# Last units of the first batch ahead of three weight tiles and of the second batch's maxima

## The chip, the core and the metric

The kernel runs on one core of one Trainium2 chip. The metric is the device time of one execution in microseconds. Before the change three runs took 1084.18 us (median), 1084.15 and 1089.09. TensorE (PE) does the matmuls, VectorE (DVE), ScalarE (ACT) and GpSimd (POOL) the elementwise work, SyncE (SP) issues nearly all DMAs. Each engine takes its instructions in the order in which they stand in its own queue.

## The reference

Attention over a window of 32 neighbours, with 32 global tokens, in 8 batches of 8 heads, 512 local tokens, 64 columns per head; then two matrices with a softplus between them, in float32:

```python
s_g = scale * q_g @ k_all.T          # 32 global tokens against all 544 keys
out_g = softmax(s_g) @ v_all
s_l = concat(scale * q_l @ k_g.T,    # each local token: 32 global keys ...
             where(abs(i - j) <= 32, scale * q_l @ k_l.T, -1e9))   # ... and its window
out_l = softmax(s_l) @ concat(v_g, v_l)
x = concat(out_g, out_l)             # 4352 rows of 512 (8 heads x 64)
h = x @ w_in                         # 512 x 2048
g = max(h, 0) + log1p(exp(-abs(h)))
out = g @ w_out                      # 2048 x 512
```

## The kernel before

**Precision.** A float32 operand is split into a high half, stored as float32r (`xh`, `gh`, the first half of a weight tile) and the remainder (`xl`, `gl`, the second half). Each product is three matmuls: high by high, low by high, high by low.

**First batch.** Batch 0 is done by special steps: for each pair of heads m = 0 to 3 and each half a = 0, 1 a local unit, and two global units between them, ten in all (`steps`). A unit goes through seven functions: `scores0` (matmuls, row maximum, exponential), `invert0`, `diag0`, `turn0`, `evict0`, `values0` (matmuls into a PSUM bank `o0_m_a` of the pool `ps_h`, which has two banks), `split0` (reads this bank: ScalarE casts it to `xh`, line L226, and VectorE subtracts to `xl`, L228). A global unit ends with ScalarE's copy to `yg` (L269). The loop over k from -2 to n + 1 (n = 10) runs units in a pipeline: in iteration k unit k + 2 begins and unit k - 2 ends.

**Weight tiles.** The weights come as 32 tiles, `wi0` to `wi15` and `wo0` to `wo15`, in the order of `order_w`: wi0, wi1, wi2, wi3, wo0, wo1, wi4, wi5, wo2, wo3, wi6, wi7, wo4, wo5, wi8 and so on. They arrive as 64-bit floats, and each is made into two halves: ScalarE's `abs_w` (L479), four VectorE operations in `bits_w` (L486, L488, L489, L492), ScalarE's cast (L497) and GpSimd's subtraction (L498). In the loop above one tile is prepared per iteration (`held`: `abs_w` in one, the rest in the next), the first twelve (`W_PRE`) of them. The rest follow between the products, when `weights(upto)` is called with a growing number.

**Other batches.** The pairs of heads m = 4 to 31 are cut into pieces with a place on one scale (`pieces`): three `scores(m, p)` at 12m + 4p, three `values(m, p)` at 22 more, `invert` and `normalise` behind them. The piece of the third `scores` also holds `maxima(m)` (GpSimd copies L329, VectorE L332 to L339) and three `probs(m, q)` (VectorE's transpose to `mb`, L347, GpSimd's subtractions L352 to L355, ScalarE's exponential L356). The pool tag `mb` has two buffers, which `abs_w` also uses for tiles below 8. The loop places the pieces of m = 4 and 5 below a limit among its last four iterations; the rest are taken after each product, as far as their place goes.

**Products.** `moe_items` puts for each batch and each of 16 blocks f the first product `h` (`hpart`, into the two `ps_h` banks), `act` (softplus: ScalarE L540 to L542, VectorE's L543, which is the last to read the `h` bank, `gh` on ScalarE, `gl` on GpSimd, L547) and the second products `o` a block or two behind. `split_x` makes `xh` and `xl` (L451, L452) of a later batch at its start; parts 1 and 3 are VectorE's.

**Order.** The program is written in one sequence, and a scheduler then orders each engine's queue by the sequence and its own estimates. In the loop, a few chains (`keep`, `note`) are forced into the written order. The single `a` bank of `ps_a` is shared by the scores of m = 6 on (`s_ps`) and by `values` (`v_ps`); VectorE's L374 and L375 are the last to read a `v_ps`.

Of the kernel before, what the change touches and what calls it, by code (L numbers as in the profile page):

```python
# [23 lines left out]
NPC = 3  # L24
# [6 lines left out]
M0 = 4  # L31
# [5 lines left out]
W_PRE = 12  # L37
START = 69
# [9 lines left out]
def windows(ap2d, start, stride, count, width):  # L48
    base = ap2d[:, start:start + width]
    return bass.AP(base.tensor, base.offset, [list(base.ap[0]), [stride, count], [1, width]])  # L50
# [3 lines left out]
def moe_over_global_local_attention(  # L54
# [219 lines left out]
    def load(m, p):  # L274
        w = QW[p] + KWID[p]
        raw = pl.tile([P, 544], F32, tag="raw", name=f"raw{m}_{p}", bufs=3)
        order["load"] = nc.sync.dma_start(out=raw[:, :w], in_=qk[m - M0, :, EW[p]:EW[p] + w]).ins
        st["raw", m, p] = raw

    def load_v(m):  # L280
        t = pl.tile([P, 2, 6, 66], F32, tag="v", name=f"v{m}", bufs=2)
        nc.gpsimd.memset(t[:, :, :, D:D + 1], 1.0)
        nc.sync.dma_start(out=t[:, :, :, 0:D], in_=v[m - M0].rearrange("p (h c d) -> p h c d", h=2, d=D))
        st["v", m] = t
# [35 lines left out]
    def grid(t, start, *dims):  # L320
        base = t[0:32, start:start + 1]
        return bass.AP(base.tensor, base.offset, [list(base.ap[0])] + [list(d) for d in dims])
# [3 lines left out]
    def maxima(m):  # L326
        mt = st.pop(("mt", m))
        for a in range(1, 4):
            nc.gpsimd.tensor_copy(mt[0:32, GW * a:GW * a + GW], mt[32 * a:32 * a + 32, 0:GW])  # L329
        e0 = 4 * GW  # L330
        for u, du, off in ((0, 1, -2), (3, 1, 3)):
            nc.vector.tensor_reduce(grid(mt, e0 + u, (7, 6), (du, 2)), grid(mt, 3 + u, (12, 6), (du, 2), (off, 2), (GW, 4)), axis=AX.XY, op=ALU.max)  # L332
        nc.vector.tensor_reduce(grid(mt, e0 + 2, (7, 6), (4, 2)), grid(mt, 3 + 2, (12, 6), (7, 2), (GW, 4)), axis=AX.X, op=ALU.max)
        g = e0 + 44
        nc.vector.tensor_reduce(grid(mt, g, (1, 2)), grid(mt, 3 + 5, (36, 2), (12, 3), (3, 2), (GW, 4)), axis=AX.XYZ, op=ALU.max)
        nc.vector.tensor_copy(grid(mt, e0 + 5, (21, 2), (7, 3)), mt[0:32, g:g + 2].unsqueeze(2).to_broadcast([32, 2, 3]))
        e = mt[:, e0:e0 + 44]
        for a in range(1, 4):
            i = nc.vector.tensor_copy(e[32 * a:32 * a + 32, 0:42], e[0:32, 0:42]).ins  # L339
        order["maxima"] = i  # L340
        st["e", m] = e

    def probs(m, p):
        s, e = st["s", m, p], st["e", m]
        k = QW[p] // 32
        mb = pl.tile([P, 2, 288], F32, tag="mb", name=f"mb{m}_{p}", bufs=2)
        nc.vector.transpose(mb[:, :, :QW[p]].rearrange("p h (s k) -> p h s k", k=32),  # L347
                            windows(e, 7 * p, 21, 2, k).unsqueeze(3).to_broadcast([P, 2, k, 32]))
        for h in range(2):
            if p < 2:  # L350
                sw = s[:, h].rearrange("p (c w) -> p c w", w=192)
                nc.gpsimd.tensor_tensor(sw, sw, windows(mb[:, h], 0, 96, 2, 192), op=ALU.subtract)  # L352
        if p == 2:
            nc.gpsimd.tensor_tensor(s[:, :, 0:192], s[:, :, 0:192], mb[:, :, 0:192], op=ALU.subtract)
            nc.gpsimd.tensor_tensor(s[:, :, 192:288], s[:, :, 192:288], mb[:, :, 96:192], op=ALU.subtract)  # L355
        nc.scalar.activation(s, s, AF.Exp, scale=0.125)  # L356

    def values(m, p):
        s, vt = st.pop(("s", m, p)), st["v", m]
        ps = ps_a.tile([P, 2, 512], F32, tag="a", name=f"v_ps{m}_{p}")  # L360
        parts = ((0, 0, 192), (192, 96, 192 if p < 2 else 96))
        for h in range(2):
            for i, (o, qs, w) in enumerate(parts):
                mm(ps[:65, h, qs:qs + w], lhsT=vt[:, h, 2 * p + i, 0:65], rhs=s[:, h, o:o + w],
                   start=i == 0, stop=i == 1, skip_group_check=True)

        if p == 0:
            st["x", m] = pl.tile([65, 2, 608], F32, tag="x", name=f"x{m}", bufs=2)
            nc.scalar.copy(st["x", m][:, :, 0:288], ps[0:65, :, 0:288])
            return  # L370
        x, o = st["x", m], XOFF[p]
        w = QW[p] if p < 2 else 160
        nc.scalar.copy(x[:, :, o + 64:o + w], ps[0:65, :, 64:w])
        nc.vector.tensor_tensor(x[:, :, o:o + 64], x[:, :, o:o + 64], ps[0:65, :, 0:64], op=ALU.add)  # L374
        nc.vector.tensor_tensor(x[:, :, 160:192], x[:, :, 160:192], ps[0:65, :, 160:192], op=ALU.add)  # L375
# [5 lines left out]
    def combine(m):  # L381
        nc.sync.dma_start(out=rec_dram[2 * m:2 * m + 2], in_=st["x", m][64:65])

        rows = rec_dram[2 * m:2 * m + 2].rearrange("h (s k) -> (h s) k", k=32)
        sc = pl.tile([38, 32], F32, tag="sc", name=f"sc{m}", bufs=1)
        nc.sync.dma_start(out=sc, in_=rows)
        st["sc", m] = sc, rows

    def invert(m):
        sc, rows = st.pop(("sc", m))  # L390
        after(nc.vector.tensor_scalar(sc, sc, 1e-9, None, op0=ALU.add), "scores")
        nc.vector.reciprocal(sc, sc)
        nc.sync.dma_start(out=rows, in_=sc)
        rb = pl.tile([64, 2, 608], F32, tag="rb", name=f"rb{m}", bufs=1)
        r = rec_dram[2 * m:2 * m + 2]
        nc.sync.dma_start(out=rb, in_=r.unsqueeze(0).to_broadcast([64, 2, 608]))
        st["rb", m] = rb

    def normalise(m):
        b, j = divmod(m, H // 2)  # L400
        x, rb = st.pop(("x", m)), st.pop(("rb", m))
        y = xa[b, j] = pl.tile([P, 608], F32, tag="xa", name=f"xa{b}_{j}", bufs=4)
        for h in range(2):
            after(nc.vector.tensor_tensor(y[64 * h:64 * h + 64], x[0:64, h], rb[:, h], op=ALU.mult), "scores")  # L404
        nc.sync.dma_start(out=xg_dram[j, :, SG * b:SG * b + SG], in_=y[:, 160:192])
        ready.add((b, j))

    def end(m):
        return 12 * m + 8 + LAG

    def pieces():
        def piece(*fs):
            def go():
                for f in fs:
                    f()
            return go
        ps = []
        for m in range(M0, M):
            for p in range(NPC):
                fs = [lambda m=m, p=p: scores(m, p)]  # L420
                if m + 1 < M:
                    fs.append(lambda m=m, p=p: load(m + 1, p))
                if p == 2:
                    fs.append(lambda m=m: maxima(m))
                    fs += [lambda m=m, q=q: probs(m, q) for q in range(NPC)]
                ps.append((12 * m + 4 * p, piece(*fs)))
                fs = [lambda m=m, p=p: values(m, p)]
                if p == 2:
                    fs.append(lambda m=m: combine(m))
                    if m + 2 < M:  # L430
                        fs.append(lambda m=m: load_v(m + 2))
                    ps.append((end(m) + STEP, lambda m=m: invert(m)))
                    ps.append((end(m) + 2 * STEP, lambda m=m: normalise(m)))
                ps.append((12 * m + 4 * p + LAG, piece(*fs)))
        ps.sort(key=lambda t: t[0])
        return ps
# [170 lines left out]
    wk = [0, 0]  # L607
# [23 lines left out]
    pcs = pieces()  # L631
# [5 lines left out]
    n = len(steps)  # L637

    def stage(k, f):
        if 0 <= k < n:  # L640
            steps[k][0][f](*steps[k][1])

    tight, held = True, None
    for k in range(-2, n + 2):
        stage(k + 2, 0)

        while k >= n - 2 and pcs[0][0] < min(12 * M0 + 8 * (k - n + 3), START):
            pcs.pop(0)[1]()
        if k == 0:
            key_masks()  # L650
        if held:
            r = bits_w(*held)
        stage(k + 2, 1)
        stage(k - 2, 5)
        stage(k - 2, 6)
        stage(k, 3)
        stage(k, 4)
        stage(k + 2, 2)
        if held:
            halves_w(*held[:2], r)  # L660
            held = None
        if -1 <= k and wk[1] < W_PRE:
            held = order_w[wk[1]]
            held += (abs_w(*held),)
            wk[1] += 1
# [78 lines left out]
```

## Time and profile before

| | |
|---|---|
| median of three runs | 1084.18 us (1084.15 to 1089.09) |
| profiled execution: time | 1085.38 us |
| profiled execution: span from first to last instruction | 1083.2 us |
| mean granted TensorE clock | 0.973 |
| TensorE busy | 1020.1 us (94%) |
| VectorE, ScalarE, GpSimd busy | 599.8, 546.8, 460.3 us |

Times in the rows are microseconds from the span's start. A row of the timeline gives start, length, engine, line, operation, what is written and read (names without buffer numbers), shape, and in brackets the idle time just before and what ended it. TensorE's ends are modelled, so a busy TensorE need not run at its peak; the granted clock says how fast it was allowed to go.

### The profile page before, as it was taken

The page shows a single profiled execution, that of the slowest core. Times are in us where ns is not written, and L with a number is a line of the kernel's source. Part 1 is how long each engine was busy: PE and PEld are TensorE (multiplying, and loading weights), DVE is VectorE, ACT ScalarE, POOL GpSimd, SP SyncE. Part 2 cuts the span into 40 slices and gives each one's busy share as a digit, 9 for nine tenths or more (in the row PEclk, how much of TensorE's full clock was granted, in tenths as well). Part 3 has the DMA queues.
Part 4 walks back from the last instruction along what each step waited for, and adds up shares of the span by engine and source line. Part 5 has one row for each costly group of instructions (what it writes and reads, how often), then busy time and mean ns, then how long its engine had stood idle before and what let it go on. Part 6 is the DMA issues. An engine that isn't in the chain of part 4 may idle for free.

```text
span 1083.2 us, 14191 instructions
## 1 busy us (share of the span) xinstructions
PE 1020.1 (94%) x5108; PEld 806.4 (74%) x5108; DVE 599.8 (55%) x1138; ACT 546.8 (50%) x968; POOL 460.3 (42%) x526
## 2 busy tenths in 40 slices
PE   6896789899999999999999999999999999999996
PEld 4774567677777777777777777777777778888895
DVE  5988697875455655565555645565556652311211
ACT  6855556544445544545444544554554544454452
POOL 2236475652444444444444344444445442322221
PEclk8998889999999999999999999999999999999998
DMA  9532332313121212123122312122122210100010
GB/s 363 161 101 88 112 129 70 93 47 95 46 57 50 85 52 57 48 56 96 48 56 57 94 47 57 48 81 57 49 55 57 85 28 13 57 15 1 1 40 19
DMA packets 78565, 75.05 MB, mean 69 GB/s; under 512 B 53380, under 2 KB 57476, under 8 KB 78496
## 3 DMA queue, kind: packets, MB, share of 16 engines
q1 hardware_dynamic: 77952, 74.09, 23.1%
q8 instruction: 40, 0.66, 0.3%
q14 instruction: 29, 0.24, 0.1%
q10 hardware_dynamic: 544, 0.07, 0.0%
HBM read 64.43 MB, written 9.71 MB: 68 GB/s over the span
## 4 chain that ended last, share of the span: by engine, by line
PE 74%; DVE 7%; DMA 4%; issue 3%; POOL 2%; ACT 1%; DVEq 0%; POOLq 0%; ACTq 0%
PE h L126 31%; PE o L126 30%; PE v_ps L126 8%; PE s_ps L126 5%; DMA rb<-rec_scratch 2%; DVE xa L404 1%; DVE xl L452 1%; DMA rec_scratch<-sc 1%; POOL s L352 1%; DVE xh L451 1%; DVE s L315 1%; POOL wo L498 0%; DVE mb L347 0%; DVE wbitswo L489 0%; DVE wbitswo L486 0%
## 5 line engine op out<-in xcount | busy, mean ns | idle before, releaser
L126 PE MATMUL h<-xh,wi 128*128 128x512 f32 (+1 forms) x1152 | 357.6, 394 | 23.1 <-DVE xl L228 9.2
L126 PE MATMUL o<-wo,gh 128*128 128x512 f32 x1088 | 348.0, 401 | 0.0
L547 POOL TENSOR_TENSOR gl<-e,gh 128x512 fp32r<-128x512 f32 x136 | 177.2, 1303 | 397.1 <-ACT gh L546 352.3
L126 PEld LDWEIGHTS h<-xh,wi 128*128 128x128 f32 x1152 | 208.8, 190 | 71.8 <-issue 16.1
L126 PEld LDWEIGHTS o<-wo,gh 128*128 128x128 f32 x1088 | 202.4, 190 | 44.3 <-issue 3.8
L126 PE MATMUL h<-xl,wi 128*128 128x512 f32 (+1 forms) x576 | 220.8, 383 | 2.8 <-DVE xl L452 2.8
L126 PE MATMUL o<-wo,gl 128*128 128x512 f32 x544 | 215.3, 396 | 0.0
L540 ACT ACTIVATE e<-h 128x512 f32<-128x512 f32 x136 | 81.4, 598 | 264.5 <-PE h L126 258.8
L543 DVE SCALAR_TENSOR_TENSOR e<-h,e 128x512 f32<-128x512 f32 x136 | 93.2, 685 | 183.6 <-ACT e L542 183.6
L352 POOL TENSOR_TENSOR s<-s,mb 128x384 f32<-128x384 f32 x112 | 138.8, 1270 | 14.0 <-DVE mb L347 14.0
L546 ACT CAST gh<-e 128x512 fp32r<-128x512 f32 x136 | 84.2, 619 | 94.2 <-DVE e L543 94.1
L126 PEld LDWEIGHTS h<-xl,wi 128*128 128x128 f32 x576 | 109.5, 190 | 27.5 <-DVE xl L452 5.6
L126 PEld LDWEIGHTS o<-wo,gl 128*128 128x128 f32 x544 | 103.5, 190 | 23.2
L126 PE MATMUL v_ps<-s,v 128*65 128x192 f32 (+1 forms) x672 | 116.6, 317 | 4.0 <-DVE s L315 3.6
L126 PEld LDWEIGHTS v_ps<-s,v 128*65 128x65 f32 x672 | 90.7, 140 | 28.3 <-DVE s L315 4.1
L315 DVE TENSOR_TENSOR s<-s_ps,mask 128x768 f32<-128x768 f32 (+1 forms) x96 | 64.9, 696 | 82.7 <-PE s_ps L126 82.7
L542 ACT ACTIVATE e<-e,one 128x512 f32<-128x512 f32 x136 | 98.5, 724 | 3.3
L356 ACT ACTIVATE s<-s 128x768 f32<-128x768 f32 (+1 forms) x84 | 66.6, 792 | 65.5 <-POOL s L352 51.4
L126 PE MATMUL s_ps<-raw 64*128 64x192 f32 (+1 forms) x672 | 78.6, 347 | 11.4 <-issue 6.8
L541 ACT ACTIVATE e<-e 128x512 f32<-128x512 f32 x136 | 85.7, 630 | 3.4
L126 PEld LDWEIGHTS s_ps<-raw 64*128 64x128 f32 x672 | 53.2, 188 | 42.4 <-issue 33.0
L316 DVE TRANSPOSE_TENSOR_REDUCE mt<-s 128x24 f32<-128x768 f32 (+1 forms) x84 | 76.2, 908 | 11.4 <-ACT s L311 9.3
(144 smaller groups left out, 831.2 us busy)
## 6 DMA issues: line engine op xcount, KB each, us to landing
raw<-in_qk SPq DMA_DIRECT2D x56, 272.0 KB
v<-in_v SPq DMA_DIRECT2D x28, 384.0 KB
out<-ot SPq DMA_DIRECT2D x34, 256.0 KB
rb<-rec_scratch SPq DMA_DIRECT2D x28, 304.0 KB
wiraw<-in_w_in SPq DMA_DIRECT2D x16, 512.0 KB
woraw<-in_w_out SPq DMA_DIRECT2D x16, 512.0 KB
raw<-in_qk SPq DMA_DIRECT2D x28, 224.0 KB
v<-in_v SPq DMA_DIRECT2D x4, 512.0 KB
```

The lines of the kernel that those rows point to most:

```text
L126: order["pe"] = after(nc.tensor.matmul(*a, **k), "pe").ins
L315: nc.vector.tensor_tensor(s[:, :, o:o + w], ps[:, :, o:o + w], mk.unsqueeze(1).to_broadcast([P, 2, w]), op=ALU.add)
L316: order["scores"] = nc.vector.tensor_reduce(windows(mt, 3 + 12 * p, 36, 2, nb), s.rearrange("p h (b k) -> p h b k", k=32), axis=AX.X, op=A ...
L352: nc.gpsimd.tensor_tensor(sw, sw, windows(mb[:, h], 0, 96, 2, 192), op=ALU.subtract)
L356: nc.scalar.activation(s, s, AF.Exp, scale=0.125)
L404: after(nc.vector.tensor_tensor(y[64 * h:64 * h + 64], x[0:64, h], rb[:, h], op=ALU.mult), "scores")
L540: nc.scalar.activation(e, ph, AF.Abs)
L541: nc.scalar.activation(e, e, AF.Exp, scale=-1.0)
L542: nc.scalar.activation(e, e, AF.Ln, bias=one)
L543: nc.vector.scalar_tensor_tensor(e, ph, 0.0, e, op0=ALU.max, op1=ALU.add)
L546: nc.scalar.copy(gh, e)
L547: nc.gpsimd.tensor_tensor(gl, e, gh.bitcast(F32), op=ALU.subtract)
```

## The change

It makes three edits. The piece of the third `scores` loses `maxima` and `probs`, which become a piece of their own half a place later (12m + 8.5). The loop places only pieces with a whole place, so the maxima of m = 4 and 5 are left for the first call behind the loop's end. And a weight tile is begun in iterations 0 to 8 in place of -1 to 10: nine tiles, wi0 to wo2; wo3, wi6 and wi7 are left for `weights`, which reaches them in the second block of batch 0.

```diff
+                ps.append((12 * m + 4 * p, piece(*fs)))
                 if p == 2:
-                    fs.append(lambda m=m: maxima(m))
-                    fs += [lambda m=m, q=q: probs(m, q) for q in range(NPC)]
-                ps.append((12 * m + 4 * p, piece(*fs)))
+                    fs = [lambda m=m: maxima(m)] + [lambda m=m, q=q: probs(m, q) for q in range(NPC)]
+                    ps.append((12 * m + 4 * p + 0.5, piece(*fs)))
...
-        while k >= n - 2 and pcs[0][0] < min(12 * M0 + 8 * (k - n + 3), START):
-            pcs.pop(0)[1]()
+        if k >= n - 2:
+            for pc in [pc for pc in pcs if pc[0] < min(12 * M0 + 8 * (k - n + 3), START) and pc[0] % 1 == 0]:
+                pcs.remove(pc)
+                pc[1]()
...
-        if -1 <= k and wk[1] < W_PRE:
+        if 0 <= k < n - 1 and wk[1] < W_PRE:
```

TensorE's queue holds the same instructions in the same order in both programs. Three places in the other queues follow.

VectorE at the end of the first batch, before. `mt_763` are the maxima of m = 5 and `mb_0_839` the first transpose made from them; `wbitswi_798` is wi6, `wbitswi_1011` and `_1057` are wi8 and wi9; the last row is the last local unit's `split0`:

```order
L335 TENSOR_REDUCE mt_763<-mt_763 32x2
L486 TENSOR_SCALAR wbitswi_798<-wbitswi_798 128x512
L336 COPY mt_763<-mt_763 32x6
L488 TENSOR_SCALAR wbitswi_798<-wbitswi_798 128x512
L339 COPY mt_763<-mt_763 32x42 x3
L486 TENSOR_SCALAR wbitswi_1011<-wbitswi_1011 128x512
L489 SCALAR_TENSOR_TENSOR wbitswi_798<-wiraw_160,wbitswi_798 128x512
L486 TENSOR_SCALAR wbitswi_1057<-wbitswi_1057 128x512
L347 STREAM_TRANSPOSE mb_0_839<-mt_763 128x576
L488 TENSOR_SCALAR wbitswi_1011<-wbitswi_1011 128x512
L492 SCALAR_TENSOR_TENSOR wiraw_160<-wiraw_160,wbitswi_798 128x512
L228 TENSOR_TENSOR xl_3_780<-o_3_1_858,xh_3_779 64x256 x2
```

And now, where `mb_2_851` is the third transpose of m = 4 and `mt_728` the maxima of m = 5:

```order
L316 TENSOR_REDUCE mt_728<-s_2_786 128x2x9
L347 STREAM_TRANSPOSE mb_2_851<-mt_647 128x2x192
L228 TENSOR_TENSOR xl_3_745<-o_3_1_791,xh_3_744 64x256 x2
L332 TENSOR_REDUCE mt_728<-mt_728 32x6x2 x2
L333 TENSOR_REDUCE mt_728<-mt_728 32x6x2
L335 TENSOR_REDUCE mt_728<-mt_728 32x2
L336 COPY mt_728<-mt_728 32x6
L339 COPY mt_728<-mt_728 32x42 x3
L486 TENSOR_SCALAR wbitswi_1011<-wbitswi_1011 128x512
```

The last unit's L228 has moved ahead of the maxima of m = 5, of wi6 and of the first operations of wi8 and wi9. On ScalarE L226 has likewise moved ahead of two `abs_w`, and L269 to the place right behind the second exponential of m = 4.

GpSimd behind the first batch, before (`gl_0` to `gl_2` are low halves of blocks 0 to 2, `wi_891` is wi7, `wi_1017` wi8, `wo_959` wo4, `wi_1063` wi9, `wo_991` wo5, `wo_1103` wo6):

```order
L498 TENSOR_TENSOR wi_891<-wiraw_162,wi_891 128x512
L547 TENSOR_TENSOR gl_0_921<-e_0_915,gh_0_920 128x512
L498 TENSOR_TENSOR wi_1017<-wiraw_894,wi_1017 128x512
L498 TENSOR_TENSOR wo_959<-woraw_164,wo_959 128x512
L498 TENSOR_TENSOR wi_1063<-wiraw_896,wi_1063 128x512
L498 TENSOR_TENSOR wo_991<-woraw_166,wo_991 128x512
L547 TENSOR_TENSOR gl_1_950<-e_1_944,gh_1_949 128x512
L498 TENSOR_TENSOR wo_1103<-woraw_898,wo_1103 128x512
L547 TENSOR_TENSOR gl_2_1006<-e_2_1000,gh_2_1005 128x512
```

And now (`wi_926` and `wi_935` are wi6 and wi7, `mt_971` the maxima of m = 6):

```order
L547 TENSOR_TENSOR gl_1_950<-e_1_944,gh_1_949 128x512
L498 TENSOR_TENSOR wi_926<-wiraw_160,wi_926 128x512
L547 TENSOR_TENSOR gl_2_1006<-e_2_1000,gh_2_1005 128x512
L498 TENSOR_TENSOR wi_935<-wiraw_162,wi_935 128x512
L282 MEMSET v_1123 128x12
L498 TENSOR_TENSOR wi_1017<-wiraw_815,wi_1017 128x512
L498 TENSOR_TENSOR wo_959<-woraw_164,wo_959 128x512
L498 TENSOR_TENSOR wi_1063<-wiraw_817,wi_1063 128x512
L547 TENSOR_TENSOR gl_3_1092<-e_3_1086,gh_3_1091 128x512
L498 TENSOR_TENSOR wo_991<-woraw_166,wo_991 128x512
L498 TENSOR_TENSOR wi_1173<-wiraw_1009,wi_1173 128x512
L329 COPY mt_971<-mt_971 32x75 x3
```

The weight halves have moved behind the first low halves `gl`, and the copies for the maxima of m = 6 stand behind wi7, wi8, wo4, wi9, wo5 and wi10 (`wi_1173`).

VectorE at the start of batch 2, before (`xa_3` is the last part of the new `x`, `mb_2` the third transpose of m = 13, `s_ps_0` the scores of m = 14); the starts of batches 3 to 6 read alike:

```order
L404 TENSOR_TENSOR xa_3_3037<-x_2790,rb_3004 64x608 x2
L451 CAST xh_3_3071<-xa_3_3037 128x128
L451 CAST xh_3_3071<-xa_3_3037 128x384
L452 TENSOR_TENSOR xl_3_3072<-xa_3_3037,xh_3_3071 128x128
L347 STREAM_TRANSPOSE mb_2_2981<-mt_2823 128x2x192
L452 TENSOR_TENSOR xl_3_3072<-xa_3_3037,xh_3_3071 128x384
L315 TENSOR_TENSOR s_0_3048<-s_ps_0_3041,mask 128x768
```

And now:

```order
L404 TENSOR_TENSOR xa_3_3037<-x_2790,rb_3004 64x608 x2
L347 STREAM_TRANSPOSE mb_2_2996<-mt_2823 128x2x192
L451 CAST xh_3_3071<-xa_3_3037 128x128
L451 CAST xh_3_3071<-xa_3_3037 128x384
L452 TENSOR_TENSOR xl_3_3072<-xa_3_3037,xh_3_3071 128x128
L315 TENSOR_TENSOR s_0_3048<-s_ps_0_3041,mask 128x768
L452 TENSOR_TENSOR xl_3_3072<-xa_3_3037,xh_3_3071 128x384
```

The third transpose stands ahead of the casts, and the larger part of `xl` behind the masking of the next scores.

## The prediction

> **What bounds the kernel now.** I read the page's share of busy time first, then the clock line, then busy time by stretch, then the timeline of each engine where TensorE stands still.
>
> ```profile
> PE 1020.1 (94%) x5108; PEld 806.4 (74%) x5108; DVE 599.8 (55%) x1138; ACT 546.8 (50%) x968; POOL 460.3 (42%) x526
> 80.00:155.00 75.00, 51.83 (x238) 38.25 (x238) 60.49 (x97) 43.76 (x75) 43.20 (x44) 0.86 0.32 107
> 155.00:220.00 65.00, 58.55 (x270) 44.90 (x269) 56.21 (x94) 36.10 (x60) 41.50 (x39) 0.90 0.30 88
> 220.00:1083.00 863.00, 842.51 (x4180) 671.59 (x4178) 419.17 (x810) 412.74 (x679) 355.37 (x405) 0.99 0.19 52
> ```
>
> The first row is the page's. The others give a stretch, its length, busy time of PE, PEld, DVE, ACT and POOL, the granted clock, and DMA. TensorE (PE) fills 94% of the span, and after 220 us it is idle 20.5 us in 863. From 80 to 155 us it is idle 23.2 us in 75 and its clock is down to 0.86. So TensorE bounds the kernel, and what can be won lies at its start. In that stretch VectorE (DVE) is busy 60.5 of 75 us: its free time, 14.5 us, limits how far everything behind it can move forward.
>
> The order of TensorE's own instructions is the same in both programs. Only VectorE, ScalarE (ACT) and GpSimd (POOL) change places, and on SP's queue one small store of `xa`, that nothing in this part waits for, goes behind one load. A gain or loss can therefore come only from TensorE's waits.
>
> ```profile
> 80.06 0.43 PE L126 MATMUL o0g<-p0g1gl,v 32*128 32x64 f32 x2
> 89.72 1.19 PE L126 MATMUL h<-xh,wi 128*128 128x512 f32 x2 [9.23 <-DVE xl L228]
> 94.16 1.46 PE L126 MATMUL v_ps<-s,v 128*65 128x192 f32 x8
> 97.22 0.72 PE L126 MATMUL h<-xh,wi 128*128 128x512 f32 x2 [1.60 <-ACT yg L269]
> 100.18 0.59 PE L126 MATMUL s_ps<-raw 64*128 64x192 f32 x4
> 112.28 0.73 PE L126 MATMUL h<-xh,wi 128*128 128x512 f32 x2 [3.41 <-DVE e L543]
> 118.53 1.01 PE L126 MATMUL s_ps<-raw 64*128 64x192 f32 x4 [4.48 <-issue]
> 154.67 1.01 PE L126 MATMUL s_ps<-raw 64*128 64x192 f32 x4 [4.10 <-ACT wo L497]
> ```
>
> Start, length, and in brackets the idle time before and its end. The longest wait, 9.23 us, is for L228: the first `h` tile takes the PSUM bank of the last local unit's `o`, which L228 still has to read. The 1.60 us are the same thing for the second `h` tile and the global unit's `yg`. The waits at 112, 118 and 154 us end when VectorE gets round to reading a bank (`e`, or the `x` additions), behind weight tiles in its queue.
>
> **The change, part by part.** *The weight tiles begin one step later.* In the first steps a tile's four VectorE operations stand between two steps:
>
> ```profile
> 13.51 0.17 DVE L173 TENSOR_SCALAR sums<-sums 128x4 f32<-128x4 f32 x1 [1.95 <-ACT e L167]
> 14.90 0.17 DVE L165 TENSOR_SCALAR sums<-sums 128x4 f32<-128x4 f32 x1
> 15.78 0.43 DVE L486 TENSOR_SCALAR wbitswi<-wbitswi 128x512 f32<-128x512 f32 x1 [0.71 <-ACT wbitswi L479]
> 17.43 0.69 DVE L492 SCALAR_TENSOR_TENSOR wiraw<-wiraw,wbitswi 128x512 int32<-128x512 int32 x1
> 18.04 0.16 DVE L173 TENSOR_SCALAR sums<-sums 128x4 f32<-128x4 f32 x1
> ```
>
> From 15.78 to 18.04 a tile takes 2.26 us, with 0.71 before it. A step without a tile waits 1.95 us for ScalarE's exponentials, so the step after the row at 14.90 (ends 15.07) goes on at 17.0 and not at 18.04: 1.0 us; the later steps keep their tile, of lower number, and get the rest back. I take 2.0 us of lead at the end of the front, with 1.0 and 2.8 as bounds. DMA hides under it: the load order stands.
>
> *The last unit ahead of wi6 and of the second maxima (m = 5).*
>
> ```profile
> 79.56 0.54 DVE L347 STREAM_TRANSPOSE mb<-mt 128x384 f32<-128x384 f32 x1
> 82.30 0.53 DVE L332 TENSOR_REDUCE mt<-mt 32x12 f32<-32x96 f32 x2 [2.20 <-POOL mt L329]
> 87.33 1.48 DVE L492 SCALAR_TENSOR_TENSOR wiraw<-wiraw,wbitswi 128x512 int32<-128x512 int32 x1
> 88.73 0.85 DVE L228 TENSOR_TENSOR xl<-o,xh 64x256 fp32r<-64x256 f32 x2
> 79.52 0.84 ACT L356 ACTIVATE s<-s 128x768 f32<-128x768 f32 x1 [2.75 <-POOL s L352]
> 82.73 0.73 ACT L226 CAST xh<-o 64x256 fp32r<-64x256 f32 x2
> 96.74 0.43 ACT L269 COPY yg<-o0g 64x64 f32<-64x64 f32 x2
> ```
>
> Now L228 follows the `mb` of 79.56, and L226 follows the L356 of 79.52. With 2.0 us of lead that L356 starts at 77.5 and is done at 78.3; L226 ends at 79.0 and L228 (0.85, its first half beside L226) at about 79.6. The matmuls of 80.06 end at 80.49, now at 78.5. TensorE then waits 1.2 us where it waited 9.23, and the first `h` tile starts at 79.7 instead of 89.72: a lead of 10.0 us. L269 now stands right behind the next exponential, so the 1.60 us go as well. The clock adds something: the first pair after the long wait took 1.19 us, that after 1.60 us of waiting 0.72. The whole first tile loses 1.5 us to the low clock: from 89.72 to 94.16 it took 4.4 us, the second from 97.22 to 100.18 only 3.0.
>
> [...]
>
> *What that lead is worth later.* wo3, wi6 and wi7 now come after the first products begin. TensorE reads wo3 only in the second products of f = 3, after the `h` tiles f = 4 and 5 that follow the `s_ps` of 118.53, and wi6 and wi7 for f = 6, just ahead of the `s_ps` of 154.67: around 124 and 129 us with the lead, while by the queues below the three are done before 116. They cost nothing by themselves. But VectorE's and GpSimd's work is the same in all, and the two get in each other's way:
>
> ```profile
> 74.43 1.29 POOL L498 TENSOR_TENSOR wo<-woraw,wo 128x512 fp32r<-128x512 f32 x1 [2.05 <-issue]
> 89.63 1.57 POOL L498 TENSOR_TENSOR wi<-wiraw,wi 128x512 fp32r<-128x512 f32 x1
> 89.95 1.79 DVE L489 SCALAR_TENSOR_TENSOR wbitswi<-wiraw,wbitswi 128x512 int32<-128x512 int32 x1
> L489 DVE SCALAR_TENSOR_TENSOR wbitswo<-woraw,wbitswo 128x512 int32<-128x512 int32 x12 | 12.4, 1034 | 0.2
> 134.33 0.53 DVE L332 TENSOR_REDUCE mt<-mt 32x12 f32<-32x96 f32 x2
> ```
>
> L489 of 89.95 ends at 91.74, 0.54 after the GpSimd operation of 89.63 does; over 80 to 220 us (fourth row) one takes 1034 ns, where L492, the same kind of operation, took 0.69 undisturbed at 17.43. So the two take turns, and VectorE's 14.5 us are not all to be had. In the new order GpSimd's copies of m = 6's maxima stand behind six weight halves, so the L332 of 134.33, which needs them, becomes late. I followed the queues from the new start. VectorE and GpSimd alternate over the second maxima until about 94 us. From there on twelve GpSimd operations (1.29 us, the row at 74.43) and eight weight tiles (2.26 us) come ahead of that L332: 15.5 + 18.1 = 33.6, one after the other, so 127.6; with some waits 129.6. From 134.33 it was 20.3 us to the `s_ps` of 154.67; some of GpSimd's work that lay in between (the last subtractions, two weight halves) now lies behind it, and I take 16 to 18. So that `s_ps` starts at 143 to 147, a lead of 8 to 11 us. Bounds: 14.5 (VectorE never idle) and 4.7 (everything keeps step with that L332 at 129.6). I take 10, what the first `h` tile has gained; VectorE has 8.8 us free from 155 to 220 to hold it there.
>
> *The maxima as a piece of their own, later on.* At the starts of batches 2 to 6 the second half of `xl` (L452) moves behind L315, and the third `mb` ahead of the casts.
>
> ```profile
> 358.37 5.04 POOL L352 TENSOR_TENSOR s<-s,mb 128x384 f32<-128x384 f32 x4
> 359.28 2.31 DVE L404 TENSOR_TENSOR xa<-x,rb 64x608 f32<-64x608 f32 x2 [0.81 <-DMA rb<-rec_scratch]
> 361.69 1.94 DVE L451 CAST xh<-xa 128x128 fp32r<-128x128 f32 x2
> 363.75 0.57 DVE L347 STREAM_TRANSPOSE mb<-mt 128x384 f32<-128x384 f32 x1
> 364.25 0.52 DVE L452 TENSOR_TENSOR xl<-xa,xh 128x384 fp32r<-128x384 f32 x1
> 364.69 0.95 DVE L315 TENSOR_TENSOR s<-s_ps,mask 128x768 f32<-128x768 f32 x1
> 364.40 1.23 POOL L354 TENSOR_TENSOR s<-s,mb 128x384 f32<-128x384 f32 x1 [0.99 <-DVE mb L347]
> 364.82 0.50 PE L126 MATMUL h<-xl,wi 128*128 128x512 f32 x1 [0.40 <-DVE xl L452]
> PE h L126 <- DVE xh L451: 6.1, 5, 1.4
> PE h L126 <- DVE xl L452: 2.0, 5, 0.4
> ```
>
> TensorE waits there five times for `xh` and then for `xl`, 8.1 us in all (the last two rows); this is on the path. The third `mb` costs nothing ahead of the casts: they wait for GpSimd anyway until 363.41, its cover. L452 gains the 0.50 us of `mb` and loses the 0.94 of L315: +0.4. L354 now starts earlier and can hold it up: +0.55 if it waits for L354's end, +1.4 if GpSimd also gets in ahead of the first part of `xl`. I take 0.6, near the row's own order: 5 x 0.6 = +3.0 us, bounds 1.8 and 7.
>
> [...]
>
> **Sum.** -10.0 + 3.0 = -7.0 us. The profiled execution has a span of 1083.2 and a time of 1085.38; both would be 7 lower (1076.2, 1078.4). It stands 1.2 above the median of the runs, 1084.18, which becomes 1077.2.
>
> **Rivals.** *The lead is given back (chance 0.22):* VectorE and GpSimd alternate until 220 us and TensorE's waits grow at the places of 118.53 and 154.67. For it speaks VectorE's 60.5 of 75 us, against it the 14.5. A lead of 3 to 5, starts of 3 to 5: 1082 to 1085. *The lead grows (0.15):* TensorE's idle time was 23.2 us, and the starts of batches hide their cost behind GpSimd: -13 to -15 and +1 to +2, 1069 to 1073. *Slower (0.05):* the third `mb` needs the buffer that GpSimd's second subtraction frees; if that ends after L404, the casts wait too. It ended about half way through the 5.04 us of the row at 358.37, so near 360.9, some 0.7 us before L404 ends at 361.59. Should each start cost over 2 us, five cost 10 and more; with a lead of 5 that is +5, 1089. It decides once the start costs more than a fifth of the lead. *Nothing happens (0.03),* since TensorE's order is unchanged: 1084; against it the 9.23.
>
> **Numbers.** The forecast has 0.55, with 1073 to 1081 as its own range. 1070 to 1083 leaves out the slower case and the end of the growing one. A change under 0.5%, 5.4 us, is about what a measurement of this kernel can't tell from none: faster needs under 1078.8. Of the forecast's 0.55 three quarters, 0.41, lie there, with the growing lead 0.56; same 0.39 (the rest of the forecast, the lead given back, and no effect), slower 0.05.
>
> **What will show it.** The first `h` matmul at 79 to 81 us with a wait of 1 to 2 us behind `o0g`, and its first pair at about 0.7. The waits of 9.23 and 1.60 gone, the `s_ps` waits near 104 and 144 still there and the second one longer. `h` waits for `xl` at five batch starts of 0.9 to 1.3 instead of 0.4. Wrong: if the front has no lead (first `h` at 82), if TensorE stands still over 10 us between 95 and 150, or if the five starts cost 2 us each.

## The result and the profile after

The changed kernel takes 1097.38 us (median of six runs, 1093.86 to 1099.85) against 1084.16 for the kernel before: the ratio is 1.0112, with a 95% interval of 1.0089 to 1.0134. It is slower by 1.1%; the forecast was faster by 0.6%. The profiled execution took 1099.85 us, the longest of these runs, with a span of 1097.9.

The page's busy row and the three stretches, in the columns that were shown for the kernel before:

```profile
PE 1029.8 (94%) x5108; PEld 813.8 (74%) x5108; DVE 613.9 (56%) x1138; ACT 546.6 (50%) x968; POOL 460.8 (42%) x526
80.00:155.00 75.00, 58.06 (x267) 43.52 (x266) 72.03 (x109) 47.50 (x82) 48.82 (x46) 0.89 0.38 121
155.00:220.00 65.00, 54.35 (x252) 42.30 (x251) 54.61 (x88) 33.74 (x57) 39.55 (x40) 0.92 0.27 76
220.00:1097.00 877.00, 848.53 (x4175) 675.65 (x4173) 427.55 (x809) 412.64 (x677) 354.11 (x405) 0.98 0.18 51
```

From 80 to 155 us TensorE does more than before (58.06 us busy instead of 51.83). Behind 220 us it needs 14 us more for the rest, is busy 6 us longer, and its granted clock is 0.98 instead of 0.99. The loss lies in the long steady part that the change seemed hardly to touch. TensorE's waits in the first batches, from its timeline:

```profile
82.71 0.70 PE L126 MATMUL h<-xh,wi 128*128 128x512 f32 x2 [1.55 <-DVE xl L228]
106.72 0.60 PE L126 MATMUL s_ps<-raw 64*128 64x192 f32 x4 [3.41 <-ACT wbitswo L479]
149.09 1.01 PE L126 MATMUL s_ps<-raw 64*128 64x192 f32 x4 [7.25 <-ACT e L541]
```

The 9.23 us ahead of the first `h` tile are 1.55. That tile starts 7.0 us earlier (82.71 for 89.72), the `s_ps` of 154.67 starts 5.6 us earlier. Much of this lead is gone by batch 1: between 155 and 245 us TensorE stands still for 14.2 us instead of 9.3. Then comes the start of batch 2, first before, then after:

```profile
359.99 0.73 PE L126 MATMUL h<-xh,wi 128*128 128x512 f32 x2
363.69 0.73 PE L126 MATMUL h<-xh,wi 128*128 128x512 f32 x2 [1.37 <-DVE xh L451]
365.16 0.62 PE L126 MATMUL o<-wo,gh 128*128 128x512 f32 x2
```

```profile
358.63 0.73 PE L126 MATMUL h<-xh,wi 128*128 128x512 f32 x2
362.70 0.73 PE L126 MATMUL h<-xh,wi 128*128 128x512 f32 x2 [1.74 <-DVE xh L451]
365.05 0.80 PE L126 MATMUL h<-xl,wi 128*128 128x512 f32 x1 [1.62 <-DVE xl L452]
365.64 1.05 PE L126 MATMUL o<-wo,gh 128*128 128x512 f32 x2
```

Here the changed kernel is still 1.36 us ahead (358.63 for 359.99). TensorE then stands still for 3.36 us instead of 1.77, and the matmuls behind take 1.05 a pair instead of 0.62. At the end of the span it is 14.7 us behind, so about 16 us are lost from here on. Five such starts, batches 2 to 6, follow. Busy time of TensorE and its granted clock in the 14 us from the start of each first `h` tile, before and after:

```profile
359.00:373.00 14.00, 12.23 (x62) 1.00 0.25 84
476.00:490.00 14.00, 12.37 (x52) 0.88 0.16 50
595.00:609.00 14.00, 12.37 (x62) 1.00 0.27 96
712.00:726.00 14.00, 12.49 (x52) 0.88 0.23 74
830.00:844.00 14.00, 12.50 (x64) 1.00 0.28 96
```

```profile
358.00:372.00 14.00, 10.64 (x39) 0.76 0.09 22
480.00:494.00 14.00, 10.64 (x41) 0.88 0.09 26
600.00:614.00 14.00, 10.65 (x42) 0.88 0.08 24
720.00:734.00 14.00, 10.64 (x38) 0.76 0.09 22
841.00:855.00 14.00, 10.64 (x45) 0.88 0.08 21
```

The third number is busy time, the one behind the bracket the clock. In these stretches the clock reads 1.00, 0.88 or 0.76. In slices of 1 us the granted clock of the changed kernel reads 0.50 from 365 to 371 us (0.65 in the slice ahead, 0.94 in the one behind), and it is 1.00 there in the kernel before. In slices of 0.5 us the second start reads 0.50 from 487.5 to 490.5 us, with 0.68 ahead and 0.91 behind; the other three, and the two of before with 0.88, read 0.50 in the same way for 3 us, or 6 where the clock is 0.76. So a step of 0.12 over 14 us is 3.4 us at half speed (0.12 x 14 / 0.5), which costs 1.7 us of work. Before, two such stretches fell into the five starts; after, seven (0.76 is two). That gives 5 x 1.7 = 8.5 us. The idle time in the five stretches grows from 8.0 to 16.8 us (70 less the sum of busy times), by 8.7. Together 17.2, against about 16 us lost.

Why TensorE waits longer is seen on VectorE and GpSimd at the start of batch 2, after:

```profile
353.56 0.67 DVE L543 SCALAR_TENSOR_TENSOR e<-h,e 128x512 f32<-128x512 f32 x1
354.98 1.57 DVE L339 COPY mt<-mt 32x42 f32<-32x42 f32 x3
357.95 2.67 DVE L404 TENSOR_TENSOR xa<-x,rb 64x608 f32<-64x608 f32 x2
361.15 1.50 DVE L451 CAST xh<-xa 128x128 fp32r<-128x128 f32 x2
362.57 1.09 DVE L452 TENSOR_TENSOR xl<-xa,xh 128x128 fp32r<-128x128 f32 x1
363.58 0.94 DVE L315 TENSOR_TENSOR s<-s_ps,mask 128x768 f32<-128x768 f32 x1
364.45 0.54 DVE L452 TENSOR_TENSOR xl<-xa,xh 128x384 fp32r<-128x384 f32 x1
355.02 1.29 POOL L547 TENSOR_TENSOR gl<-e,gh 128x512 fp32r<-128x512 f32 x1 [1.74 <-ACT gh L546]
357.44 4.99 POOL L352 TENSOR_TENSOR s<-s,mb 128x384 f32<-128x384 f32 x4 [1.13 <-DVE mb L347]
362.39 1.12 POOL L354 TENSOR_TENSOR s<-s,mb 128x384 f32<-128x384 f32 x1
```

Before, two of these rows read:

```profile
356.44 0.56 DVE L339 COPY mt<-mt 32x42 f32<-32x42 f32 x3
363.55 0.28 DVE L452 TENSOR_TENSOR xl<-xa,xh 128x128 fp32r<-128x128 f32 x1
```

The first `xl` subtraction takes 1.09 us instead of 0.28 while GpSimd's L354 (362.39 to 363.51) is under way; L315 then stands ahead of the second. And the three L339 copies take 1.57 us instead of 0.56: they end just behind GpSimd's L547 (at 356.31), which came sooner because `e` of the last hidden tile (L543) now stands ahead of most of the maxima. The later copies make the first `mb`, and with it the L352s, later. The casts of `xh` end 0.22 us behind the last L352 in both kernels (362.65 behind 362.43, before 363.63 behind 363.41), so the rows point to this as the source of the longer wait for `xh`.

### The profile page after: what moved, and what is told of

It reads as the page before. It is cut to its first block, busy times and chain, and to the rows that moved or that the text cites. A ratio compares the mean times of both kernels' runs of the same rounds, so it can differ in the third digit from the quotient of the medians.

```text
span 1097.9 us, 14187 instructions
## 1 busy us (share of the span) xinstructions
PE 1029.8 (94%) x5108; PEld 813.8 (74%) x5108; DVE 613.9 (56%) x1138; ACT 546.6 (50%) x968; POOL 460.8 (42%) x526
## 4 chain that ended last, share of the span: by engine, by line
PE 73%; DVE 17%; issue 4%; ACT 2%; DMA 2%; POOL 1%; ACTq 0%; POOLq 0%; DVEq 0%
PE o L126 30%; PE h L126 29%; PE v_ps L126 8%; PE s_ps L126 5%; DVE xa L404 2%; DVE xl L452 2%; DMA rb<-rec_scratch 1%; ACT e L167 1%; DVE s L315 1%; DVE wbitswo L489 1%; DVE mt L339 1%; DVE wbitswi L489 1%; DVE e L543 1%; DVE mb L347 1%; DVE wbitswo L486 1%
## 5 line engine op out<-in xcount | busy, mean ns | idle before, releaser
L126 PE MATMUL h<-xh,wi 128*128 128x512 f32 (+1 forms) x1152 | 357.2, 394 | 15.1 <-DVE xh L451 11.5
L547 POOL TENSOR_TENSOR gl<-e,gh 128x512 fp32r<-128x512 f32 x136 | 178.6, 1313 | 420.2 <-ACT gh L546 371.5
L126 PE MATMUL o<-wo,gh 128*128 128x512 f32 x1088 | 352.6, 406 | 0.0
L126 PEld LDWEIGHTS o<-wo,gh 128*128 128x128 f32 x1088 | 205.8, 194 | 45.4 <-issue 4.0
L543 DVE SCALAR_TENSOR_TENSOR e<-h,e 128x512 f32<-128x512 f32 x136 | 93.1, 685 | 184.8 <-ACT e L542 184.7
L352 POOL TENSOR_TENSOR s<-s,mb 128x384 f32<-128x384 f32 x112 | 138.1, 1264 | 16.7 <-DVE mb L347 16.7
L126 PEld LDWEIGHTS h<-xl,wi 128*128 128x128 f32 x576 | 109.8, 191 | 33.6 <-DVE xl L452 11.7
L126 PE MATMUL v_ps<-s,v 128*65 128x192 f32 (+1 forms) x672 | 119.1, 322 | 2.1 <-DVE s L315 2.1
L315 DVE TENSOR_TENSOR s<-s_ps,mask 128x768 f32<-128x768 f32 (+1 forms) x96 | 65.0, 696 | 84.1 <-PE s_ps L126 84.1
L374 DVE TENSOR_TENSOR x<-x,v_ps 65x128 f32<-65x128 f32 x56 | 15.8, 282 | 121.9 <-ACT x L373 121.9
```

The source lines that it names most:

```text
L126: order["pe"] = after(nc.tensor.matmul(*a, **k), "pe").ins
L315: nc.vector.tensor_tensor(s[:, :, o:o + w], ps[:, :, o:o + w], mk.unsqueeze(1).to_broadcast([P, 2, w]), op=ALU.add)
L543: nc.vector.scalar_tensor_tensor(e, ph, 0.0, e, op0=ALU.max, op1=ALU.add)
L547: nc.gpsimd.tensor_tensor(gl, e, gh.bitcast(F32), op=ALU.subtract)
```

## The experiments

Microseconds are medians. Kernels that ran at different times are compared by their ratios to the kernel before, run beside them on the same chip (1084 to 1086 us); a difference of ratios is turned into microseconds by 1084. The edits are shown shortened, some with plainer names; `...` stands for code left out.

**The parts alone.** The theory: the starts lose the time. The rival: the three tiles that come later do. First the nine tiles alone:

```diff
-        if -1 <= k and wk[1] < W_PRE:
+        if 0 <= k < n - 1 and wk[1] < W_PRE:
```

> The kernel before with the third edit alone: nine weight tiles in the loop instead of twelve, the maxima as before. Its order of work in batches 2 to 6 is that of the kernel before. Theory S (the five starts of batches 2 to 6 lose the time: there the split of the third xa waits longer, 3.4 us of standstill a start instead of 1.8, with half-clock matmuls behind it, 3.2 us a start, 16 in all): the front's small gain of 1.2 us is all that is left, 1083 us (1081.5 to 1084.5), and the first matmuls of h2_0 wait 1.3 to 1.4 and 0.4 us as before. Rival W (the three weight tiles that come later are what costs, through POOL and DVE in the first two batches): 1090 to 1098.

It took 1077.9 us (0.9933, interval 0.9921 to 0.9946), faster than expected by either theory. On all engines its order of work is the one that the whole change gives when only the pairs 4 and 5 have pieces of their own. So this is the forecast's kernel without the reordered starts. Its first `h` tile, its worst wait and two of its starts (the other three have 1.00, 1.00 and 0.88):

```profile
79.81 0.70 PE L126 MATMUL h<-xh,wi 128*128 128x512 f32 x2 [1.55 <-DVE xl L228]
146.14 1.01 PE L126 MATMUL s_ps<-raw 64*128 64x192 f32 x4 [7.34 <-ACT e L541]
```

```profile
354.00:368.00 14.00, 12.37 (x61) 1.00 0.29 97
470.00:484.00 14.00, 12.46 (x52) 0.88 0.16 51
```

The `s_ps` of 154.67 is 8.5 us early, and the starts stand still as briefly as before.

The pieces of their own from pair 6 on, in the kernel before:

```diff
-                if p == 2:
-                    fs.append(lambda m=m: maxima(m)) ...
+                late = [maxima(m), probs(m, 0), probs(m, 1), probs(m, 2)]
+                alone = m >= 6    # else: with the scores, as before
```

> The kernel before with the first edit for the pairs 6 to 31 alone: maxima and probabilities as a piece of their own, half a step behind their scores; the loop with its twelve tiles and the pairs 4 and 5 as before. Theory S: the five starts cost 16 us, 1098 to 1101, with h waits of 1.7 and 1.6 us at each start. Rival W: no cost, 1083 to 1085. If the cost needs both (the starts only meet the longer wait because the first batch's lead shifts them): between, about 1090.

It took 1101.01 us (1.0150, 1.0131 to 1.0169): the cost does not need the other edits. Then the same pieces on top of the nine tiles, cut in two, for the pairs up to 11 (`m < 12`) and from 12 on (`m >= 12`):

> The changed kernel, with the maxima of the pairs 12 to 31 back in the piece of their scores: those of the pairs 4 to 11 alone are pieces of their own. The order in the batches 2 to 6 is that of the kernel before, and up to there that of the changed kernel. Theory S (two separate costs: the starts 16 us, and in the first batch the lead that the split of the pairs 6 to 8 gives back, 4.5 us by the first matmuls of h1): 1077.9 + 2.5 to 4.5 = 1080 to 1083. Rival (the lead of the nine tiles differs from run to run, and the split gives nothing back): 1077 to 1079. Rival (the starts' cost hangs on when they are reached, and not on their order): 1090 or more.

> The kernel with nine tiles in the loop, and with the maxima of the pairs 12 to 31 alone as pieces of their own: the first two batches in the order that gave 1077.9, the starts of batches 2 to 6 in that of the changed kernel. Theory S: 1077.9 + 16 = 1094 (1091 to 1096), h waits of 1.7 and 1.6 us at each start. Rival (the starts only cost what they do behind the changed front): 1078 to 1085.

The first took 1079.83 us (0.9941, 0.9918 to 0.9963), not told apart from the nine tiles alone; the 2.5 to 4.5 us were not found. The second took 1095.46 us (1.0073, 1.0047 to 1.0098). Its starts read as in the changed kernel (seven slow stretches); the first of them:

```profile
353.00:367.00 14.00, 10.66 (x37) 0.76 0.09 22
```

The reordered starts cost 1.0073 - 0.9933, 15 us, on the good front, and 1.0112 - 0.9941, 18.5 us, in the whole change. Rival W fell.

**Which reordering at the starts.** In the changed kernel the second `xl` subtraction back ahead of L315:

```diff
+        if j == 3 and b > 1:         # in normalise, ahead of the next scores
+            split_x(b, 3)            # sets order["xl"] to its last subtraction
...
-                nc.vector.tensor_tensor(s..., ps..., mask, op=ALU.add)
+                after(nc.vector.tensor_tensor(s..., ps..., mask, op=ALU.add), "xl")
```

> The changed kernel, in which at the five starts alone the second xl subtraction of the third xa (128 x 384) stands ahead of the mask addition of the next scores (L315) on VectorE, as in the kernel before; the third transpose of mb stays ahead of the xh casts. Theory S1 (the mask addition ahead of xl is the main part): the wait for xl falls from 1.62 to about 0.7 us, and with less standstill the half clock behind it goes in most starts: 1097.4 - 5 x (0.9 + 1.6) = 1085 (1084 to 1088). S1 without the clock: 1097.4 - 5 x 0.9 = 1093. Rival S2 (the transpose ahead of the casts is the main part, with the lock between VectorE and GpSimd behind it): 1096 to 1098.

It took 1090.54 us (1.0049, 1.0030 to 1.0067), a gain of 7 us, between the two. The wait for `xl` fell to 1.15 us only: the two subtractions take 1.96 us together (0.80 before) while GpSimd's L354 and L355 are under way (1.75 us). This lengthening is all that the rows show of what S2 calls a lock. The clock was 0.88 at each of the five starts, so five slow stretches instead of seven. What is left over the kernel without reordered starts, 1.0049 - 0.9941 or 11.7 us, goes with the earlier `mb` and the earlier `e`; `mb` alone was not put back.

The opposite, in the kernel with nine tiles, L315 ahead of the second `xl` subtraction and nothing else moved:

```diff
-            nc.vector.tensor_tensor(lo, f(t), hi, op=ALU.subtract)
+            after(nc.vector.tensor_tensor(lo, f(t), hi, op=ALU.subtract), "masked")   # 128x384 of xl3
```

> The kernel with nine tiles (1077.9), in which at the five starts alone the mask addition of the next scores (L315) stands ahead of the second xl subtraction of the third xa; the third transpose of mb and e1_15 stay where they were. The wait for xl should grow from 0.4 to 1.2 to 1.3 us, the standstill from 1.6 to 2.5. If the standstill alone costs: 1077.9 + 5 x 0.9 = 1082. If more than about 2 us of standstill brings the half clock at each start, not in two of five: another 3 x 2, 1086 to 1090.

```profile
358.82 0.73 PE L126 MATMUL h<-xh,wi 128*128 128x512 f32 x2 [1.24 <-DVE xh L451]
360.99 0.50 PE L126 MATMUL h<-xl,wi 128*128 128x512 f32 x1 [1.45 <-DVE xl L452]
```

```profile
355.00:369.00 14.00, 11.32 (x56) 1.00 0.25 86
473.00:487.00 14.00, 11.31 (x45) 0.88 0.16 50
592.00:606.00 14.00, 11.31 (x47) 0.88 0.14 41
711.00:725.00 14.00, 11.42 (x48) 0.88 0.11 32
831.00:845.00 14.00, 11.32 (x44) 0.88 0.15 46
```

It took 1087.01 us (1.0022, 1.0009 to 1.0035), 9.6 us more than with nine tiles alone. The wait for `xl` grew by 1.05 us, which is 5.3 us at five starts; two more slow stretches are 3.4. One exchange of two instructions thus costs 1.9 us a start, twice the 0.94 of L315, with the clock at 0.88 at four starts instead of two. Here, with `mb` back behind the casts, L354 starts later (359.53) and the first `xl` subtraction (358.68) takes 0.28 us again.

In the changed kernel, `e` of the last hidden tile behind the maxima again:

```diff
-            nc.vector.scalar_tensor_tensor(e, ph, 0.0, e, ...); gh; gl
+            late.append(...)      # f == 15, b = 1 to 5: behind the next pieces, after "maxima"
```

> The changed kernel; at the five starts alone the step max(h,0)+e of the last hidden tile (e1_15 to e5_15, L543) is held behind the four copies that end the maxima on VectorE, so GpSimd gets its subtraction for gl later. The rest of VectorE's order stays. Theory L (the three copies L339 take 1.57 us instead of 0.56 since they meet that subtraction): the copies return to 0.6 us, the casts of xh end 1.0 us sooner, the standstill falls from 3.36 to some 2.4 us and the half clock behind it in part: 1097.4 - 5 x 1 to 2 = 1087 to 1092. Rival G (the subtraction then lands on the xa products and the casts, which lengthen by as much): 1096 to 1099.

It took 1095.83 us (1.0093, 1.0065 to 1.0121): rival G. The copies do return to 0.56 us, but GpSimd's subtraction then falls among the L352s and the products for `xa` take longer, 3.24 us for 2.67:

```profile
347.97 0.56 DVE L339 COPY mt<-mt 32x42 f32<-32x42 f32 x3
351.26 3.24 DVE L404 TENSOR_TENSOR xa<-x,rb 64x608 f32<-64x608 f32 x2 [0.66 <-DMA rb<-rec_scratch]
352.01 1.84 POOL L555 TENSOR_TENSOR gl<-e,gh 128x512 fp32r<-128x512 f32 x1
356.58 0.73 PE L126 MATMUL h<-xh,wi 128*128 128x512 f32 x2 [2.03 <-DVE xh L451]
```

**The clock.** The changed kernel with matmuls that add zero during the standstill, on 32 rows:

```diff
+    for _ in range((8, 7)[i // 2]):    # ahead of xh3 and of xl3
+        mm(ph, lhsT=ident[0:32], rhs=mask[0:32, 32:33].to_broadcast([32, 512]), start=False, stop=False)
```

> The changed kernel with matmuls that add zero to h in the standstill of the five starts: 8 ahead of the first matmul on xh of the third xa, 7 ahead of the one on its xl (32 rows, 512 columns each, some 0.23 us at full clock). The waits are as in the changed kernel. Theory C (half of the loss is the half clock behind the standstill, 8 us of 16): 1087 to 1091, a granted clock near 1.00 in the stretches of the five starts. Rival D (the standstill alone costs and the clock is no part): 1096 to 1099. If the added matmuls are longer than the waits: 1100 or more, with no idle time ahead of the h groups.

1096.63 us (1.0102, 1.0089 to 1.0116): the time of rival D, but not for its reason. TensorE was busy without a gap, and the clock fell all the same (0.88, 0.88, 0.76, 0.88, 0.88); two of the five:

```profile
356.00:370.00 14.00, 14.00 (x59) 0.88 0.13 43
596.00:610.00 14.00, 14.00 (x53) 0.76 0.14 40
```

So the matmuls were made to fill the array, in the bank of the next `h` tile:

```diff
+    for _ in range(7):                 # ahead of xh3 and of xl3
+        mm(h_next, lhsT=wi[0][:, 0, fs], rhs=xh[0], start=True, stop=True)
```

> The changed kernel with matmuls in the standstill of the five starts, now over the whole array: 7 and 7 products of wi0 and the first xh, 128 rows by 512 columns, into the bank of the next h tile, whose own first matmul overwrites them. The 32-row matmuls before left the clock at half behind them. Theory C2 (a full array keeps the clock, and the half clock is about half of the loss): 1086 to 1091, matmuls of o behind the start at 0.23 us. Rival D (the clock falls all the same, so the wait itself isn't what lowers it): 1095 to 1099.

```profile
353.00:367.00 14.00, 13.80 (x66) 1.00 0.23 80
```

It took 1085.55 us (0.9998, 0.9986 to 1.0011), with a clock of 1.00 at all five starts. VectorE's operations there take as long as in the changed kernel (2.66, 1.53, 1.10, 0.94 and 0.54 us from L404 to the second `xl`), and 12.4 us are back: seven slow stretches of 1.7 us are 11.9. To tell rows from zeros, the same matmuls on the first 32 rows (`wi[0][0:32, 0, fs]`, `xh[0][0:32]`):

> The changed kernel with the 7 and 7 matmuls of the run that kept the full clock, but on 32 of the 128 rows of the same tiles, and the same columns and bank. If the rows are what counts for the clock: about 0.92 granted in the five stretches as with the 32-row matmuls of zeros, and 1095 to 1098. If the zeros were what let the clock fall: clock 1.00 and about 1085.

```profile
471.00:485.00 14.00, 14.00 (x50) 0.76 0.19 60
593.00:607.00 14.00, 14.00 (x56) 0.88 0.14 40
```

The five clocks were 1.00, 0.76, 0.88, 0.76 and 0.88, the time 1096.15 us (two runs; 1.0098, 1.0062 to 1.0133). On 32 rows real data does not keep the clock either, so between this run and the one before it the rows make the difference, 10.8 us. Zeros on 128 rows were not run.

**The front.** The first two edits for the pairs 4 and 5 alone, with all twelve tiles:

```diff
+                alone = m < 6     # and the loop places whole-number pieces only; twelve tiles, as before
```

> The kernel before with the first two edits for the pairs 4 and 5 alone: their maxima and probabilities as pieces of their own behind the loop, all twelve tiles in the loop. If the nine tiles are what brings the lead: 1082 to 1086, no change. If the maxima behind the loop free VectorE for the last subtractions of the first batch by themselves: first h near 80 to 82 and 1077 to 1080.

It took 1074.35 us (0.9894, 0.9875 to 0.9913), with the first `h` tile at

```profile
81.46 0.70 PE L126 MATMUL h<-xh,wi 128*128 128x512 f32 x2 [1.50 <-DVE xl L228]
```

So moving the maxima brings the lead by itself, 11.5 us. The nine tiles on top of it cost 4; that order is the one of the nine tiles alone. These bring a lead by themselves too (7.3 us), and moving the maxima of the pairs 4 and 5 then changes no queue. With ten tiles, wi6 and wi7 later and wo3 not (`-1 <= k < n - 1`):

> The kernel with the maxima of the pairs 4 and 5 behind the loop (1074.4), with ten tiles in the loop instead of twelve: wi6 and wi7 come behind it, wo3 stays. If each tile that comes later costs about the same (3.5 us for the three of the change): 1076 to 1077.5. If only the tiles that fall between the maxima and the first products cost, wi6 and wi7 with them: 1077 to 1079. If they cost nothing and the 3.5 us are between executions: 1073 to 1075.

1076.89 us (0.9934, 0.9912 to 0.9956), as with nine. If the 4 us are a cost and not scatter (this interval and that of the twelve tiles, up to 0.9913, just meet), wi6 and wi7 make it, not wo3.

**Versions that beat both.** Full-array matmuls in the standstills of the starts of batches 1 to 6, 12 and 3 at the first, 5 and 1 at the others, with nine tiles:

> The kernel with nine tiles in the loop (1077.9) and, in the standstill at the starts of batches 1 to 6, matmuls over the whole array into the bank of the next h tile, as many as the waits there hold: 12 and 3 at h1_0, 5 and 1 at h2_0 to h6_0. If the half clock behind a standstill is a cost of its own here too (two of the five starts show a granted clock of 0.94 to 0.95 in that kernel, some 1.7 us each, and the start of batch 1 some 1.5): 1073 to 1076. If they only come on top of the waits: 1078 to 1081.

1073.11 us (0.9878, 0.9855 to 0.9901), 6 us better than without them. With the maxima behind the loop and twelve tiles:

> The kernel with the maxima of the pairs 4 and 5 behind the loop and all twelve tiles in it (1074.4), with the added full-array matmuls at the starts of batches 1 to 6 (12 and 3, then 5 and 1). That kernel shows the half clock behind the start of batch 1 and behind one of the five others. If front and starts are separate costs, which add up: 1074.4 less 2 to 5, so 1069 to 1073. If the gain of the full clock came in the other kernel from a front that happened to be early: 1074 to 1076.

1070.07 us (0.9868, 0.9851 to 0.9886), the fastest kernel of the study. The gain over the same kernel without them is 2.8 us by the ratios, at the low end; the intervals overlap.

## Why the prediction was wrong

**The step that failed** is the price of the five starts: "I take 0.6, near the row's own order: 5 x 0.6 = +3.0 us, bounds 1.8 and 7." They cost 15 to 18.5; no run shows the 0.6. Of this 8.7 are longer waits, 1.7 a start where 0.6 was taken, and the rest is the half clock behind them, which the sum did not have at all. A second term was too large: the lead, 10.0 in the sum, was about 7 without the starts. The first error is 12 to 15.5 us, the second about 3, of the 19 between forecast and result.

- The waits. "+0.4" for L315 was near: its 0.94 made 1.05 us where L315 alone was moved, without the gain from the moved `mb`. "The third `mb` costs nothing ahead of the casts" held for the casts, which still end 0.22 us behind the L352s. But the earlier `mb` lets L354 start sooner, and the first part of `xl` takes 1.09 us instead of 0.28. This was named as the +1.4 case and given up for 0.6; the wait for `xl` grew by 1.22. The move of `e` ahead of the maxima was not priced; it makes the copies longer (1.57 us for 0.56), and the wait for `xh` grew by 0.4 at the start of batch 2, though holding it back only moved the collision.
- The clock. The prediction weighs it at the front alone and names no clock for the starts. The trace of before had the sign: 0.88 at two of five starts, with waits of 1.6 and 1.5 us in all. At the front the pair behind a wait of 1.55 us took 0.70, as forecast. At the starts with L315 alone moved, two waits of 2.6 to 2.7 us in all (1.24 and 1.45 at the first, with 0.73 us of matmuls between them) went with 0.88 at four starts of five and with 1.00 at the first. The length of the waits alone does not tell which start the half clock follows.
- The rival "slower" had the right direction and the right condition ("should each start cost over 2 us"), with a time 8 us too low (1089), but by luck: its mechanism was a wait for a buffer, and the third `mb` follows L404 without a wait (360.65 behind 360.62). It had a chance of 0.05.

**What held.** The order alone moved TensorE's waits. The first `h` tile started 1.55 us behind a wait (1.2 forecast), its first pair took 0.70, and the 1.60 us for `yg` are gone. The `s_ps` waits are still there, at 106.72 and 149.09 (104 and 144 were named), and the second is longer, 7.25 us for 4.10; the first is shorter, 3.41 for 4.48. Without the starts the same order took 1077.9 us, where 1077.2 was forecast; that the two are so near is luck, since the starts did not cost the +3.0 there and the lead was about 7, not 10. All three signs of being wrong came in the profiled execution: the first `h` later than 82, 13.4 us of standstill between 95 and 150, and starts of over 2 us. But the kernel with nine tiles stands still for 14.3 us between 95 and 150 and is faster, so the second sign told nothing.

**What was mis-sized.** The lead at the front, "2.0 us (1.0 to 2.8)", was -0.7 in the profiled execution, whose first `h` came at 82.71; other executions of the same order had it between 79.8 and 81.9, and twelve tiles gave 81.46, so the gain of the later beginning is about half a microsecond and lost in scatter. The lead at the `s_ps` of 154.67, "8 to 11", was 5.6 here and 8.5 with nine tiles. The L332 ahead of it was read well, at 129.1 where 129.6 was forecast, but from there to the `s_ps` it was 20.0 us (19.9 with nine tiles), not "16 to 18": that GpSimd's work moved behind it brought no gain there. "They cost nothing by themselves" (wo3, wi6, wi7) stands against 4 us for wi6 and wi7, the size of which stays uncertain. How much lead is left at the start of batch 1 scatters by about 6 us between executions with one order up to there (its first wait for `xh` ends at 243.52 in the profiled execution, at 237.13 to 241.74 in others, at 244.73 before), so a gain given back by the pairs 6 to 11 could not be shown, and why the profiled execution kept so little stays open. On SP's queue the store of `xa` went behind two loads, not one; no wait of TensorE hangs on it.

**The parts by ratio:** maxima of pairs 4 and 5 -11.5, later tiles +4.2, pairs 6 to 11 +0.9, pairs 12 to 31 +15.2 to +18.5: +8.8 to +12.1, against +12.1 measured. The upper end closes by construction, since 18.5 is taken from the whole change itself; with the 15.2 that were measured apart from it 3.3 us are left, which the intervals of the ratios don't tell from nothing, and neither do they the +0.9. The order of the parts matters: with the nine tiles taken first they bring -7.3 and the maxima nothing more.

## What to carry to other kernels

Where TensorE is the bound, price a wait by the clock behind it too (here 1.7 us for each slow stretch): read the granted clock in a stretch of some 14 us around each wait that is already there, before making it longer. When a general rule ("its own piece, for all pairs") is made for one place, look at what it reorders where nothing had to change: the pairs 4 and 5 alone, with twelve tiles, were 1.1% faster. A standstill that cannot be removed can be filled with matmuls of the full array into a bank that is overwritten later: 7 and 7 at each start brought 12.4 us in the changed kernel.

## What was new about the hardware

- The clock fell without one long gap. In one profiled execution each, two waits with 0.7 us of matmuls between them went with slow stretches of 3.4 us: waits of 2.6 to 2.7 us in all at four of five starts (L315 alone moved), of 1.5 to 1.8 us at two of five (before), and of 3.4 us at all five, with two such stretches at two of them (the changed kernel). The `s_ps` matmuls just ahead (0.92 us) use 64 rows; what they add to this was not tested.
- A TensorE that was busy without a gap (14.00 of 14 us), but for some 3.5 us of it with matmuls on 32 rows, showed the clock of the changed kernel's standstill, 0.76 to 0.88: at all five starts with zeros, at four of five with real data. With real data on 128 rows it kept 1.00 at all five.
